# A token-MLP's first matmul split into eight and six column blocks instead of seven and seven

## The chip, the core and the metric

The kernel runs on one core of a Trainium2 chip. Time is the device time of one execution in microseconds (us), as the median of several runs; a profiled execution gives a trace of every instruction. Five engines matter here: TensorE (PE, with its weight loads shown as PEld) multiplies; VectorE (DVE) and ScalarE (ACT) do elementwise work and move results out of PSUM, the matmul's accumulators, which have eight banks; GpSimd (POOL) only builds constants; SyncE (SP) issues almost all DMA transfers, in order, from one queue.

## The reference

`x` is a [2048, 512] bf16 matrix. The result mixes a linear-attention block `a` and a token-mixing MLP `b` by a gate per row:

```python
g = _sigmoid((x * gate_w).sum(-1, keepdims=True))
# a: linear attention, 32 heads of 16
q, k, v = split(x @ wqkv)
phi = lambda t: jnp.where(t > 0, t + 1, jnp.exp(t)) + 1e-6
pq, pk = phi(q), phi(k)
kv = einsum("bhsd,bhse->bhde", pk, v);  z = einsum("bhsd->bhd", pk)
a = (pq @ kv / (pq . z + 1e-6)) @ wo
# b: layer norm, then an MLP along the 2048 rows
h = _layernorm(x)
u = gelu(einsum("bsd,sf->bdf", h, w1) + b1)     # w1: [2048, 1792]
y = einsum("bdf,fs->bds", u, w2) + b2           # w2: [1792, 2048]
b = y.transpose(0, 2, 1)
return g * a + (1 - g) * b
```

(`split` stands for the reference's reshape into q, k and v of 32 heads.) Note that the MLP mixes rows: its first matmul contracts over all 2048 rows of `h`, its second makes one output row out of 1792 hidden values.

## The kernel before

The 2048 rows are 16 row tiles of 128 (`NT`), the 512 features four blocks (`ND`), the 1792 hidden columns of w1 fourteen blocks of 128 (`NF`). Every large matmul is 128 x 128 weights against 512 columns and fills one PSUM bank. The code is written under a framework that keeps each engine's instructions in the order in which the program pins them, hands out PSUM banks from one pool of eight (`bank`, L70) and inserts the waits. So five orders are fixed by hand: TensorE's, VectorE's, ACT's, SP's queue and ACT's few DMAs.

TensorE's order is this.

- Warm-up matmuls (`warm_ps`) and a small one that turns the biases (`vps`, read by ACT at L229 and L230).
- **First MLP stage** (L266 to L277): while x and w1 stream in tile by tile, every row tile t is normalised (`ln_bn`, `ln_aggr`, `ln_apply` on VectorE, a square root on ACT) into `xh`, and TensorE adds its product with the first seven blocks of w1's columns to seven accumulators `accA`, all open at once. The last four row tiles (`TAIL`) are done accumulator by accumulator, so that each is finished and sent through gelu (L257, ACT) while the next one is being completed. Columns 0 to `FA` of w1 lie in `w1A`, the rest in `w1B`.
- **k stage** (L314 to L323): per row tile, four matmuls `kacc`, `phi` (an exp on ACT, two instructions on VectorE) into `pk`, and four tiles later four matmuls that add x^T pk to four accumulators `Gps`; VectorE adds up z. `Gps` goes to `G_sb` (L331). While the first MLP stage still runs, VectorE also does twelve of the sixteen dot products of the gate (`gate`, L252).
- **Second MLP stage** (L469): one block of w1's columns at a time (`mlp1_block`, 16 matmuls, accumulator `accB`), seven in all; behind the first four stand 3, 4, 4 and 5 tiles of q (`q_tile`, 4 matmuls and `phi` each), behind the first also the small kv matmuls, behind the second those of W2sb = kv wo. The accumulators of the first four blocks are kept until the q tiles are done, then gelu'd; ACT loads its gelu table once for this.
- **Last stage** (L540): for eight, four and three row tiles at a time the second matmul of the MLP (`y_mm`, 14 matmuls), then for each of those tiles the attention's part, 4 matmuls with weights from `pqT` (`a_mm`), and `finish` on ACT, and the store. The last row tile comes by itself in two parts.

Between q and the last stage lies a path without TensorE. `normalise(t)` (L388, four instructions on VectorE) divides phi(q) by its denominator and multiplies it by the gate's odds, then SP stores the tile to `q_dram`. After four tiles `turn(c)` (L408) reads it back as four DMA transposes into `pqT`. SP's queue from L500 on is, in order: the stores of tiles 0 to 3, the two loads of the second half of w2 (`load_w2(1, ...)`), turn(0), the stores of 4 to 7, turn(1), the stores of 8 to 11, turn(2), and then output stores mixed with the last four normalised tiles. `a_mm` of tiles 4c to 4c+3 needs turn(c).

w1A, w1B and the two halves of w2 share two slots of the pool `wstream`: the first half of w2 comes into the place of w1A, the second into that of w1B, when their last matmuls are done. `load_w2(0, ...)` stands in SP's queue behind the transposes of z (`z_out`, L361).

Of the kernel before, what the change touches and what calls it, by code (L numbers as in the profile page):

```python
# [11 lines left out]
BF16 = mybir.dt.bfloat16  # L12
# [4 lines left out]
def kernel(  # L17
# [14 lines left out]
    P = nc.NUM_PARTITIONS  # L32
# [7 lines left out]
    S, D = X.shape  # L40
    F = B_w1.shape[1]
    NT = S // P
    ND = D // P
    NF = F // P
    SC = 512
    NSC = S // SC
    assert S == 2048 and D == 512 and F == 1792
    NFA = NF // 2
    FA = NFA * P
    TAIL = 4  # L50

# [7 lines left out]
    gw_row_view = gate_w.rearrange("(o d) -> o d", o=1)  # L59

    persist = ctx.enter_context(tc.tile_pool(name="persist", bufs=1))
    wpool = ctx.enter_context(tc.tile_pool(name="wstream", bufs=2))
    work = ctx.enter_context(tc.tile_pool(name="work", bufs=3))
    dpool = ctx.enter_context(tc.tile_pool(name="dpool", bufs=1, space=bass.MemoryType.DRAM))
    psum = ctx.enter_context(tc.tile_pool(name="psum", bufs=8, space=bass.MemoryType.PSUM))
# [1 line left out]
    def ptile(shape, dt, name):  # L67
        return persist.tile(shape, dt, name=name, tag=name)

    def bank(name):  # L70
        return psum.tile([P, SC], FP32, name=name, tag="bank")
# [10 lines left out]
    wk_sb = ptile([P, ND, D], BF16, "wk_sb")  # L82
# [1 line left out]
    wo_sb = ptile([P, ND, D], BF16, "wo_sb")  # L84
    pqT = ptile([P, ND, S], BF16, "pqT")
    uT = ptile([P, NF, D], BF16, "uT")
    G_sb = ptile([P, ND, D], BF16, "G_sb")
    kvbdT = ptile([P, ND, P], BF16, "kvbdT")
    pq = ptile([P, NT, D], BF16, "pq")
    zb = ptile([P, D], FP32, "zb")  # L90
# [24 lines left out]
    nc.vector.memset(eps_t[:], EPS)  # L115


    w1A = wpool.tile([P, NT, FA], BF16, name="w1A", tag="w")
    w1B = wpool.tile([P, NT, FA], BF16, name="w1B", tag="w")

    pin = tc.keep_in_program_order

    def load(o, i, eng=None, **kw):
        pin((eng or nc.sync).dma_start(out=o, in_=i, **kw))
# [113 lines left out]
    def gate(t):  # L238
        junk = work.tile([P, D], BF16, name="junk", tag="junk", bufs=1)
        tc.keep_in_program_order(  # L240
            nc.vector.tensor_tensor_reduce(  # L241
                out=junk[:], in0=xr[:, t, :], in1=gw_b[:], scale=1.0, scalar=0.0,
                op0=ALU.mult, op1=ALU.add, accum_out=gpre[:, t : t + 1],
            )
        )


    def gate_odds(t0, t1):
        pin(nc.vector.tensor_scalar_min(out=gpre[:, t0:t1], in0=gpre[:, t0:t1], scalar1=60.0))
        pin(nc.scalar.activation(out=odds[:, t0:t1], in_=gpre[:, t0:t1], func=ACT.Exp))  # L250
# [6 lines left out]
    def gelu(acc, j):  # L257
        pin(
            nc.scalar.activation(
                out=uT[:, j, :], in_=acc[:], func=ACT.Gelu_apprx_tanh,  # L260
                bias=b1_sb[:, j : j + 1], scale=1.0,
            )
        )


    accA = [bank("accA") for _ in range(NFA)]  # L266

    def mlp1(acc, w, col, t, last):
        mm(acc[:], w[:, t, col : col + P], xh[:, t, :], t == 0, last)

    for t in range(NT - TAIL):
        for j in range(NFA):
            mlp1(accA[j], w1A, j * P, t, False)
    for j in range(NFA):
        for t in range(NT - TAIL, NT):
# [49 lines left out]
    def evict(o, acc, i):  # L325
        if i % 2 == 0:
            pin(nc.scalar.copy(out=o, in_=acc))
        else:
            pin(nc.vector.tensor_copy(out=o, in_=acc))

    for i in range(ND):  # L331
        evict(G_sb[:, i, :], Gps[i][:], i)
    pin(nc.vector.tensor_copy(out=z_parts[:, 0, :], in_=zacc[:]))
# [7 lines left out]
    def mlp1_block(j):  # L341
        acc = bank("accB")
        for t in range(NT):
            mlp1(acc, w1B, (j - NFA) * P, t, t == NT - 1)
        return acc

    def q_tile(t):
        qacc = bank("qacc")
        for k in range(ND):
            mm(qacc[:], xT[:, k, t * P : (t + 1) * P], wq_sb[:, k, :], k == 0, k == ND - 1)  # L350
        phi(pq[:, t, :], qacc)
# [14 lines left out]
    def z_row():  # L366
        pin(nc.vector.tensor_reduce(out=z_cols[:], in_=z_turned[:], op=ALU.add, axis=AX.X))
        load(zr_dram[:].rearrange("o (p j) -> p (o j)", p=P), z_cols[:])
        zm = persist.tile([P, D], FP32, name="z_mixed", tag="zacc")
        z_row_mixed.append(zm)  # L370
        load(zm[:], zr_dram[:].to_broadcast([P, D]))

    def z_order():
        pin(
            nc.scalar.copy(
                out=zb[:].rearrange("p (j c) -> p j c", j=ND),
                in_=z_row_mixed[0][:].rearrange("p (c j) -> p j c", j=ND),
            )
        )
# [36 lines left out]
    def kv_blocks():  # L416
        kvps = bank("kvps")
        for j in range(ND):
            for k in range(ND):
                for p in range(0, P, 64):  # L420
                    c = j * P + p
                    mm(kvps[p : p + 64, j * 64 : j * 64 + 64], wv_sb[:, k, c : c + 64],
                       G_sb[:, k, c : c + 64], k == 0, k == ND - 1, tile_position=(0, p))

        for j in range(ND):
            for p in range(0, P, 32):
                r = (p + 32 * j) % P
                pin(
                    nc.vector.tensor_tensor(
                        out=kvbdT[r : r + 32, j, p : p + 32],  # L430
                        in0=kvps[p : p + 32, j * 64 + p % 64 : j * 64 + p % 64 + 32],
                        in1=mask[p : p + 32, p : p + 32], op=ALU.mult,
                    )
                )

    def w2_blocks():
        w2ps = [bank("w2ps") for _ in range(ND)]
        for j in range(ND):
            for p in range(0, P, 32):
                r = (p + 32 * j) % P  # L440
                mm(w2ps[j][p : p + 32, :], kvbdT[r : r + 32, j, p : p + 32],
                   wo_sb[r : r + 32, j, :], True, True, tile_position=(r, p))
        for j in range(ND):
            evict(W2sb[:, j, :], w2ps[j][:], j)


    w2s = []

    def load_w2(h, f0):
        if f0 == 0:  # L450
            w2s.append(wpool.tile([P, NF, S // 2], BF16, name="w2h", tag="w"))
        load(
            w2s[h][:, f0 : f0 + 7, :],
            w2_view[:, f0 : f0 + 7, h * (S // 2) : (h + 1) * (S // 2)],
        )


    z_out()
    load_w2(0, 0)
    load_w2(0, 7)  # L460


# [3 lines left out]
    gates = [[], [12, 13], [14, 15], []]  # L466
    qi = 0
    waiting = []
    for b in range(NFA):  # L469
        acc = mlp1_block(NFA + b)  # L470
        waiting.append((acc, NFA + b))
        if b == 0:
            kv_blocks()
        if b == 1:
            w2_blocks()
        if b < QB:
            for _ in range(n_q[b]):
                q_tile(qi)
                qi += 1
            for t in gates[b]:  # L480
                gate(t)
            if b == 2:
                gate_odds(0, NT)
            if b == 1:
                z_row()
        if b == QB - 1:
            z_order()
        if b >= QB - 1:
            for a, j in waiting:
                gelu(a, j)  # L490
            waiting = []
# [8 lines left out]
    for t in range(12):  # L500
        normalise(t)
        if t == 3:
            load_w2(1, 0)
            load_w2(1, 7)
        if t % 4 == 3:
            turn(t // 4)
# [80 lines left out]
```

## Time and profile before

| what | value |
| --- | --- |
| median of 3 runs | 163.24 us (163.14 to 163.45) |
| profiled execution | 163.19 us, of it span 161.5 us from the first to the last instruction |
| granted TensorE clock | 1.000 |
| first matmul of accA to last store | 4.96 us to 161.5 us |
| first MLP stage (accA) | 4.96 to 29.3 us |
| k stage (kacc, Gps) | 29.3 to 57.0 us |
| second MLP stage and q | 57.0 to 96.2 us |
| last stage (yps) | 96.2 to 158.5 us |
| w1A: 15 loads of 224 KB, issue to landing | 4.2 us (median) |
| w2's halves: 4 loads of 1792 KB | 7.7 us (median) |
| pqT: 16 DMA transposes, issue to landing | 2.8 us (median) |

Stages are by the start of the first matmul of each. The trace models the end of a matmul: one is shown with some 379 ns although the next starts 216 ns after it, so starts are what to count. A timeline line gives start, length, engine, line of the code, operation, what it writes and reads, and how many instructions are merged in it; a "q" behind an engine's name means its queue (waits and DMA issues). Helpers record all matmuls at L75 and all DMA issues at L124, so tiles' names tell them apart.

### The profile page before, as it was taken

What the parts mean: (1) busy time and instruction counts of PE and PEld (TensorE: products, weight loads), DVE (VectorE), ACT (ScalarE), POOL (GpSimd) and SP (SyncE); (2) the same over time, 40 slices, a digit from 0 to 9 for tenths busy, and PEclk for the clock granted to TensorE, in tenths of its full rate; (3) what the DMA queues carried; (4) which work ended last, traced back from release to release, by engine and by line L of the source; (5) the groups of instructions that cost most, each with busy time, mean ns of one, the idle gap of its engine ahead of it and who ended that gap; (6) DMA issues with size and microseconds to landing.
All of it is one profiled execution on the core that took longest, in us unless ns stands there. A gap on an engine that the chain in (4) does not pass through costs nothing.

```text
span 161.5 us, 2192 instructions
## 1 busy us (share of the span) xinstructions
PE 156.9 (97%) x775; PEld 73.0 (45%) x789; DVE 117.6 (73%) x272; ACT 53.1 (33%) x91; POOL 1.5 (1%) x10
## 2 busy tenths in 40 slices
PE   7999999999999999999999999999999999999992
PEld 5444444444444445444444444444444444444452
DVE  2999989999999997998959999999999900000002
ACT  3222258962332124261348730000008330150140
POOL 3000000000000000000000000000000000000000
PEclk9999999999999999999999999999999999999999
DMA  4999996445699942169930103999445367360021
GB/s 139 279 351 341 335 186 139 108 105 102 165 394 380 265 136 81 37 211 381 334 67 0 39 32 80 345 392 296 153 69 162 91 196 233 71 189 4 0 97 33
DMA packets 36806, 28.33 MB, mean 175 GB/s; under 512 B 20412, under 2 KB 33084, under 8 KB 36796
## 3 DMA queue, kind: packets, MB, share of 16 engines
q1 hardware_dynamic: 36320, 27.90, 58.7%
q10 hardware_dynamic: 476, 0.30, 0.6%
q8 instruction: 6, 0.10, 0.3%
q14 instruction: 4, 0.03, 0.1%
HBM read 19.28 MB, written 4.46 MB: 147 GB/s over the span
## 4 chain that ended last, share of the span: by engine, by line
PE 97%; issue 1%; DVE 0%; DVEq 0%
PE yps L75 38%; PE accA L75 15%; PE accB L75 15%; PE qacc L75 9%; PE kacc L75 9%; PE Gps L75 8%; PE warm_ps L75 2%; PE kvps L75 0%; DVE ot L531 0%; PE w2ps L75 0%; PE vps L75 0%; DVEq L531 0%
## 5 line engine op out<-in xcount | busy, mean ns | idle before, releaser
L75 PE MATMUL yps<-uT,w2h 128*128 128x512 bf16 (+2 forms) x234 | 49.0, 366 | 0.2
L75 PEld LDWEIGHTS <-w2h 128*128 128x128 bf16 x238 | 22.8, 98 | 25.9
L524 ACT ACTIVATE ot<-yps,c,c 128x512 bf16<-128x512 f32 x15 | 11.5, 777 | 46.9 <-DVE pq L400 24.4
L75 PE MATMUL accB<-xh,w1B 128*128 128x512 bf16 x110 | 24.9, 379 | 0.1
L75 PE MATMUL accA<-xh,w1A 128*128 128x512 bf16 x110 | 24.4, 381 | 0.1
L531 DVE TENSOR_SCALAR ot<-yps,c,c 128x384 bf16<-128x384 f32 (+1 forms) x2 | 1.1, 544 | 29.0 <-PE yps L75 29.0
L75 PEld LDWEIGHTS <-xT 128*128 128x128 bf16 x128 | 12.4, 98 | 14.9 <-issue 0.2
L75 PEld LDWEIGHTS <-w1B 128*128 128x128 bf16 x112 | 10.9, 98 | 13.2
L75 PEld LDWEIGHTS <-w1A 128*128 128x128 bf16 x112 | 10.9, 98 | 13.2 <-issue 0.4
L75 PE MATMUL kacc<-wk_sb,xT 128*128 128x512 bf16 x63 | 15.7, 379 | 0.1
L75 PE MATMUL Gps<-pk,xr 128*128 128x512 bf16 x62 | 15.5, 379 | 0.1
L75 PE MATMUL yps<-W2sb,pqT 128*128 128x512 bf16 (+2 forms) x67 | 14.6, 366 | 0.1
L75 PE MATMUL qacc<-wq_sb,xT 128*128 128x512 bf16 x62 | 14.4, 379 | 0.1
L282 ACT ACTIVATE e<-qacc 128x512 bf16<-128x512 f32 x16 | 9.6, 597 | 12.2 <-PE qacc L75 8.0
L282 ACT ACTIVATE e<-kacc 128x512 bf16<-128x512 f32 x16 | 9.2, 598 | 12.7 <-PE kacc L75 7.0
L196 DVE BATCH_NORM_STATS2 stats<-xr 128x6 f32<-128x512 bf16 (+1 forms) x19 | 11.1, 582 | 2.1 <-DMA xr<-in_A_x_dram 2.1
L400 DVE SCALAR_TENSOR_TENSOR pq<-pq,odds,rd 128x512 bf16<-128x512 bf16 x16 | 12.0, 752 | 0.6
L396 DVE TENSOR_REDUCE den<-prod 128x32 f32<-128x544 f32 x16 | 11.5, 720 | 0.6
L289 DVE SCALAR_TENSOR_TENSOR pk<-kacc,e 128x512 bf16<-128x512 f32 x16 | 11.1, 692 | 1.0
L289 DVE SCALAR_TENSOR_TENSOR pq<-qacc,e 128x512 bf16<-128x512 f32 x16 | 11.1, 692 | 0.6
L241 DVE CUSTOM_DVE_ANT_0 junk<-xr,gw_b 128x512 bf16<-128x512 bf16 x16 | 11.0, 690 | 0.5
L284 DVE TENSOR_SCALAR e<-e 128x512 bf16<-128x512 bf16 x32 | 9.2, 288 | 2.8 <-ACT e L282 2.4
(54 smaller groups left out, 95.3 us busy)
## 6 DMA issues: line engine op xcount, KB each, us to landing
w2h<-in_B_w_dram SPq DMA_DIRECT2D x4, 1792.0 KB, 7.7
w1B<-in_B_w_dram SPq DMA_DIRECT2D x4, 896.0 KB, 8.3
w1A<-in_B_w_dram SPq DMA_DIRECT2D x15, 224.0 KB, 4.2
xr<-in_A_x_dram SPq DMA_DIRECT2D x16, 128.0 KB, 3.9
q_dram<-pq SPq DMA_DIRECT2D x16, 128.0 KB, 1.8
out_dram<-ot SPq DMA_DIRECT2D x15, 128.0 KB, 1.8
wk_sb<-in_A_wqkv_dram SPq DMA_DIRECT2D x1, 512.0 KB, 7.0
wv_sb<-in_A_wqkv_dram SPq DMA_DIRECT2D x1, 512.0 KB, 13.5
```

The lines of the kernel that those rows point to most:

```text
L75: nc.tensor.matmul(o, lhsT=lhsT, rhs=rhs, start=start, stop=stop, **kw)
L196: pin(nc.vector.bn_stats(out=stats[t][:, h, :], in_=xr[:, t, d0:d1]))
L241: nc.vector.tensor_tensor_reduce(out=junk[:], in0=xr[:, t, :], in1=gw_b[:], scale=1.0, scalar=0.0, op0=ALU.mult, op1=ALU.add, accum_out=gp ...
L282: pin(nc.scalar.activation(out=e[:], in_=acc[:], func=ACT.Exp))
L284: nc.vector.tensor_scalar(out=e[:], in0=e[:], scalar1=1.0, scalar2=PHI_EPS, op0=ALU.min, op1=ALU.add)
L289: nc.vector.scalar_tensor_tensor(out=o, in0=acc[:], scalar=0.0, in1=e[:], op0=ALU.max, op1=ALU.add)
L396: pin(nc.vector.tensor_reduce(out=den[:], in_=prod[:], op=ALU.add, axis=AX.X))
L400: nc.vector.scalar_tensor_tensor(out=heads, in0=heads, scalar=odds[:, t : t + 1], in1=rd[:].unsqueeze(2).to_broadcast([P, NH, HEAD]), op0= ...
L524: nc.scalar.activation(out=ot[:, d0:d1], in_=yps[:, d0:d1], func=ACT.Identity, scale=c1[:, t : t + 1], bias=c2[:, t : t + 1],)
L531: nc.vector.tensor_scalar(out=ot[:, d0:d1], in0=yps[:, d0:d1], scalar1=c1[:, t : t + 1], scalar2=c2[:, t : t + 1], op0=ALU.mult, op1=ALU.add,)
```

## The change

The first MLP stage works on eight blocks of w1's columns with eight open accumulators, the second on the remaining six. `w1A` grows to 1024 columns (256 KB per row tile instead of 224) and `w1B` shrinks to 768. The two slots of `wstream` become two tags with a slot each: `w1st` for w1A and then w2's first half (32 KB per partition instead of 28), `w2nd` for w1B and then w2's second half (28 KB, as before). The 4 KB come from `G_sb`, which no longer has a place of its own but is made, where it is first written, in the place of `wk_sb`, the weights of the k stage. The loop of the second stage runs over six blocks; which q tiles, gates and other parts stand behind block b is as it was, so two blocks instead of three come after the last q tile.

```diff
-    NFA = NF // 2
+    NFA = 8
     FA = NFA * P
...
-    wpool = ctx.enter_context(tc.tile_pool(name="wstream", bufs=2))
+    wpool = ctx.enter_context(tc.tile_pool(name="wstream", bufs=1))
...
-    G_sb = ptile([P, ND, D], BF16, "G_sb")
...
-    w1A = wpool.tile([P, NT, FA], BF16, name="w1A", tag="w")
-    w1B = wpool.tile([P, NT, FA], BF16, name="w1B", tag="w")
+    w1A = wpool.tile([P, NT, FA], BF16, name="w1A", tag="w1st")
+    w1B = wpool.tile([P, NT, F - FA], BF16, name="w1B", tag="w2nd")
...
+    G_sb = persist.tile([P, ND, D], BF16, name="G_sb", tag="wk_sb")
     for i in range(ND):
         evict(G_sb[:, i, :], Gps[i][:], i)
...
-            w2s.append(wpool.tile([P, NF, S // 2], BF16, name="w2h", tag="w"))
+            w2s.append(wpool.tile([P, NF, S // 2], BF16, name="w2h", tag=("w1st", "w2nd")[h]))
...
-    for b in range(NFA):
+    for b in range(NF - NFA):
         acc = mlp1_block(NFA + b)
```

## The prediction, made before the change was run

> **What bounds the kernel now.** I read the page first (busy shares, the chain of waits), then the timeline of SP's queue, then TensorE's own timeline stage by stage.
>
> ```profile
> span 161.5 us, 2192 instructions
> PE 156.9 (97%) x775; PEld 73.0 (45%) x789; DVE 117.6 (73%) x272; ACT 53.1 (33%) x91; POOL 1.5 (1%) x10
> ...
> PE 97%; issue 1%; DVE 0%; DVEq 0%
> ```
>
> The chain that ends last is TensorE from 0.83 us to 158.5 us, with no other engine in it until the last store. A busy TensorE could still hide pauses, so I took starts, not durations: the 48 matmuls of the last three blocks of the second stage start from 85.79 to 96.15, which is 10.36/48 = 0.2158 us each, and the same spacing holds in every other stage. From 5.13 to 157.4 us TensorE never really waits. The change leaves the number of matmuls as it is (14 blocks of 16 either way), so it can win only what the head loses: the first matmul of accA waits for the first normalised tile (4.96 until the second starts at 5.35 instead of 5.18, 0.17 us), and the 29th starts 0.253 after its predecessor, 0.04 us late. Nothing else is to be had. The question is what the reordering makes late.
>
> The one place where data arrive just in time is the read of pqT in the last stage:
>
> ```profile
> 96.09 2.87 SPq L124 DMA_DIRECT2D q_dram<-pq  x2
> 99.05 1.07 SPq L124 DMA_DIRECT2D w2h<-in_B_w_dram  x2
> 100.48 10.98 SPq L124 DMA_TRANSPOSE pqT<-q_dram  x4
> 111.50 2.06 SPq L124 DMA_DIRECT2D q_dram<-pq  x4
> 114.96 6.29 SPq L124 DMA_TRANSPOSE pqT<-q_dram  x4
> 121.30 2.05 SPq L124 DMA_DIRECT2D q_dram<-pq  x4
> 124.75 5.03 SPq L124 DMA_TRANSPOSE pqT<-q_dram  x4
> ```
>
> This is SP's queue in order of time (start, length, what, how many). A line of four transposes is one turn(c). Turn(1), issued from 114.96, feeds tiles 4 to 7. Its four landings are at 117.56, 120.61, 121.10 and 122.78 (issue plus its own time to landing). Against it stands the timeline of TensorE's weight loads:
>
> ```profile
> 120.11 6.79 PEld L75 LDWEIGHTS <-pqT 128*128 128x128 bf16 x32
> ```
>
> Its 32 loads are 0.2159 apart ((6.79 - 0.10)/31), so tile 4 (loads 17 to 20) wants its four pieces at 123.57, 123.78, 124.00 and 124.21. The tightest margin is 1.43 us, at tile 4's fourth piece; every other one of this stage is 2.9 us or more.
>
> **The change, part by part.** *Eight blocks first.* 16 matmuls (block 8) move from the second stage to the first: 16 x 0.2158 = 3.45 us. Everything from the first kacc to the last qacc starts 3.45 us later. From y_mm on TensorE is where it was, since b = 6 of the second loop is gone: after the last qacc stand two blocks (6.91 us) instead of three (10.36).
>
> *The head.* Per row tile w1A has 256 KB instead of 224, so up to w1A of tile 1 64 KB more go ahead. At the 300 GB/s of 5.5 to 6.5 us that is 0.21 us: it landed at 6.54 and lands at 6.75. Its load is wanted at about 6.80 (5.35 + 7 x 0.216, less the 0.06 of a load ahead of its matmul), a wait of -0.05 to 0.15 us; I take 0.0. Later tiles have slack: 384 KB per tile at 345 GB/s are 1.11 us against 8 x 0.2158 = 1.73 us of TensorE, and a tile's layer norm on VectorE repeats every 1.18 us. The 0.04 us pause of the 29th matmul goes. Head: between -0.04 and +0.15, taken as 0.
>
> *Banks.* warm_ps, vps and seven accA are nine tiles for eight banks now; with ten, one accA must take over vps's bank, free once ACT's two copies of L229 and L230 are done at 5.93; its first matmul is due no earlier than 6.43. kacc then starts on the bank of accA[0], whose gelu (24.46 now, 2.6 later then) ends some 5 us before. The later rows: gelu of block 7 from 32.99, the table load 1.28, exp 0.60, then VectorE's 0.29 and 0.69 put pk(0) at 36.6; Gps wants it at 33.65 + 3.45 = 37.1. VectorE's gates, which end at 32.3 now, are off that path. Cost 0; if the 0.5 us of cover went, each 0.1 over it would be 0.1 on the end.
>
> *G in wk's place.* It waits for the last reader of wk_sb. The kacc matmuls end 4.3 us ahead of the last Gps (52.81 against 57.13 in the chain), and G is evicted only after Gps. Cost 0; the waits on ACT's and VectorE's queues behind it are the same ones as now.
>
> *w1B and the w2 halves.* w1B is 3.1 MB instead of 3.7 MB, starts some 1.5 us later (0.5 MB more ahead of it at 345 GB/s), ends where it did, and is wanted 3.45 us later. w2's first half is released by SP's transposes of z behind the Gps stage: 3.45 us later, in by about 85 (81.7 now, when the small transfer behind it had landed), wanted at 96.15. The row of z (z_mixed in at 85.02, wanted by ACT's copy at 86.49) moves as a whole. The second half goes where w1B was, free at 96.15 as now.
>
> *Gelus ahead of y_mm.* zb, the table load and the gelus of blocks 8 to 12 (88.91 to 91.91 now) move to 92.4 to 95.4; TensorE wants the first at 97.88. The gelu of the last block is at 96.36 either way. Cost 0, with 2.5 us of cover.
>
> *The normalise chain.* This is the part that is not covered. VectorE starts normalise(0) at 88.39, after the phi of the last qacc, which TensorE's qacc sets; so it starts at 91.84. A tile takes 2.53 us and VectorE has no pause until 128.9, so every q_dram is 3.45 us later. On SP stands behind the store of tile 3 (98.63, waiting for VectorE) first the load of w2's second half, then turn(0), the stores of 4 to 7, turn(1). That whole row moves by 3.45 us. Turn(0) then lands at 117.1, wanted at 120.11: covered. Turn(1) is issued from 118.41.
>
> How long does turn(1) take? Now 6.29 us to issue; turn(2), the same bytes, took 5.03, and the views of the tile pqT over these two stretches give
>
> ```profile
> DMA to landing us min/median/max: 2.6/3.2/4.5
> ...
> DMA to landing us min/median/max: 2.5/2.7/2.7
> ```
>
> (the first line is turn(1), the second turn(2)).
> The packet records say why: at 118.16 one 16 KB packet of the instruction queue occupies one DMA engine for 1.37 us, in the middle of turn(1). The queue's last two packets are 27.65 us apart, the time in which TensorE starts 256 instructions (128 pairs of 0.2158), so it follows TensorE's count and stays at 118.16. The last packet of the stores before turn(1) is at 114.59, hence at 118.04 then: the fetch falls between the stores and the transposes (first data at 116.20 + 3.45 = 119.65, the fetch over at 119.53). So turn(1) then has turn(2)'s rhythm: landings 2.54, 3.83, 5.21 and 6.51 after the first issue, at 120.95, 122.24, 123.62 and 124.92. The fourth is wanted at 124.21; with 0.04 from landing to load (the w1A wait at 6.58) TensorE stops for 0.75 us.
>
> [...]
>
> The bounds for this stall: 0 if SP's row gains 0.75 us, 2.06 if turn(1) keeps its present rhythm (122.78 + 3.45 + 0.04 - 124.21). I take 0.75, since the position of the fetch follows from rows. What is later is covered: turn(2) landed at 131.26 and is wanted at 139.11, turn(3) at 143.92 against 151.63, w2's second half was in by 112.1 (turn(0), behind it in the queue, had landed) and is wanted at 128.53; each moves by 3.45 at most.
>
> **Sum.** Profiled execution 163.19 us (span 161.5 and 1.7 around it), head 0, stall +0.75: 163.94. The median is 163.24, 0.05 above the profiled run: 164.0 us.
>
> **Rivals.** *Turn(1) is still hit by the fetch.* The gap between 118.04 and 118.16 is 0.12 us; a DMA row 0.15 later or a fetch 0.15 earlier puts a store behind the 1.37 us packet, SP waits for that store, and the transposes start up to 1.4 later. For it: the small gap, and ten tiles in eight banks may shift TensorE's count by a wait or two. Against: both times follow TensorE. Stall 2.06: 165.3 us.
>
> *No stall: w2's load makes it up.* This one ends on the other side.
>
> ```profile
> 100.00:104.00 4.00, 3.95 (x19) 1.84 (x19) 3.86 (x7) 0.00 (x0) 0.00 (x0) 1.00 0.83 266
> 104.00:108.00 4.00, 4.00 (x20) 1.79 (x19) 3.79 (x8) 0.00 (x0) 0.00 (x0) 1.00 1.05 395
> ```
>
> The last two columns are the share of the DMA engines and GB/s. Were the first of these stretches as fast as the second, the load would save (395 - 266) x 4 / 395 = 1.3 us; from 0.75 us on nothing waits, and the time is 163.2. Against it: the load has the engines to itself both now and after, so I see no reason for another pace.
>
> *pk(0) is late.* If ACT loads a second table behind the last gelu (1.28 us, 0.8 over the cover of 0.5), Gps waits 0.8 us on top: 164.8. Against it, one load stands there now, and the functions are the same. *Faster:* only the head's 0.04 to 0.2 us without a stall, 163.0 to 163.2; to pass 0.2% it would need more than the head holds.
>
> **Chances.** Forecast 0.55, fetch hits 0.27, no stall 0.10, late pk(0) 0.04, faster 0.04. A measurement of this kernel tells 0.2% (0.33 us) from no change. Slower: the forecast, the fetch and pk(0), 0.86; within 0.2%: 0.11, the no-stall case and a little of the faster one; faster 0.03. The range goes from a stall of 0.3 (163.5) to the fetch case with 0.2 for the head (165.5).
>
> **What would show it.** Right: the only new wait of TensorE on a DMA is a weight load of pqT near 124.2, 0.75 us long, at tile 4's last piece; normalise starts near 91.8; kacc starts near 32.8. A wait of 2 us there with a late store speaks for the fetch. Wrong: no pause of pqT, or TensorE waiting anywhere before 96 us.

## The result and the profile after

The changed kernel takes 164.21 us (median of 8 runs, 163.9 to 165.01) against 163.34 us for the kernel before (8 runs, 163.13 to 163.88): a ratio of 1.0057, 95% interval 1.0039 to 1.0075, or 0.93 us slower (0.64 to 1.23; the medians lie 0.87 apart). The profiled execution took 164.22 us, its span is 162.5 us instead of 161.5. The granted clock is 0.998 against 1.000.

From the page of the changed kernel, the span, the busy shares and the shares of the chain that ends last:

```profile
span 162.5 us, 2208 instructions
PE 157.6 (97%) x789; PEld 73.0 (45%) x789; DVE 117.8 (72%) x272; ACT 53.2 (33%) x91; POOL 1.5 (1%) x10
...
PE 71%; DVE 18%; DMA 5%; SPq 2%; issue 1%; ACTq 1%; ACT 0%; DVEq 0%
```

The busy shares are as good as unchanged and show nothing. The chain does: it was TensorE for 97%, now a quarter of it is put down to VectorE, SP's queue and DMAs. Where it comes back to TensorE is in the pieces of the chain in order of time (start, length, what):

```profile
101.40 0.75 DVE pq L401
...
111.51 0.75 DVE pq L401
...
116.19 0.36 DVE rd L399
...
116.66 1.78 DMA q_dram<-pq
...
118.46 1.35 SPq L123
...
119.86 1.25 SPq L123
...
121.16 1.26 SPq L123
...
122.47 2.92 DMA pqT<-q_dram
...
125.43 34.12 PE yps L75 x175
```

Read from below: TensorE's last 34 us hang on the fourth transpose of pqT, that one on SP's issue of the three before it (1.25 to 1.35 us each), these on the store of tile 7, which went out at 116.66 as the last of the four stores. Above the store the chain misleads, because it infers who released whom: the `rd` at 116.19 belongs to tile 9, while normalise(7) had ended with the `pq` at 111.51 (0.75 long). The four stores waited for SP's own row. Normalise(3) ended with the `pq` at 101.40, SP issued that tile's store at 102.18, then the load of w2 and turn(0) up to 114.96, then the four stores. So VectorE's late start reaches turn(1) through tile 3 and what stands behind it on SP, and VectorE's 18% is too much.

SP's queue, then TensorE's matmuls before and after, from the timelines:

```profile
102.18 0.33 SPq L123 DMA_DIRECT2D q_dram<-pq  x1
102.60 1.07 SPq L123 DMA_DIRECT2D w2h<-in_B_w_dram  x2
104.03 10.93 SPq L123 DMA_TRANSPOSE pqT<-q_dram  x4
115.00 2.06 SPq L123 DMA_DIRECT2D q_dram<-pq  x4
118.46 5.26 SPq L123 DMA_TRANSPOSE pqT<-q_dram  x4
```

```profile
120.33 7.07 PE L75 MATMUL yps<-W2sb,pqT 128*128 128x512 bf16 x31
```

```profile
120.43 4.26 PE L75 MATMUL yps<-W2sb,pqT 128*128 128x512 bf16 x19
125.43 2.98 PE L75 MATMUL yps<-W2sb,pqT 128*128 128x512 bf16 x13 [0.74 <-DMA pqT<-q_dram]
```

(One of the 32 matmuls has no record in the profile before.) From the load on, each line of SP's row is 3.50 to 3.55 us later than it was (99.05, 100.48, 111.50, 114.96), only turn(1) is quicker to issue, 5.26 us instead of 6.29. In the changed kernel TensorE stops before its 20th matmul with pqT, the fourth of tile 4. The figure in brackets, 0.74, is short of the truth, because a matmul is shown with 379 ns of which the next one overlaps all but 216. By starts, the 19th is at 124.315 and the 20th at 125.431: 1.116 - 0.216 = 0.90 us. From the first matmul of the last stage to the last of the kernel TensorE takes 62.149 us in the profile before and 63.059 now, 0.91 more. So the stall is the whole of the last stage's loss; the rest of the span's 1.0 us is 0.10 that stood on the clock already when the last stage began (96.257 instead of 96.154), and that comes from the head.

### The profile page after: what moved, and what is told of

Read it like the earlier page. It is cut to its first block, busy times and chain, and to the rows that moved or that the text cites. A ratio compares the mean times of both kernels' runs of the same rounds, so it can differ in the third digit from the quotient of the medians.

```text
span 162.5 us, 2208 instructions
## 1 busy us (share of the span) xinstructions
PE 157.6 (97%) x789; PEld 73.0 (45%) x789; DVE 117.8 (72%) x272; ACT 53.2 (33%) x91; POOL 1.5 (1%) x10
## 4 chain that ended last, share of the span: by engine, by line
PE 71%; DVE 18%; DMA 5%; SPq 2%; issue 1%; ACTq 1%; ACT 0%; DVEq 0%
PE yps L75 21%; PE accA L75 17%; PE kacc L75 9%; PE accB L75 9%; PE Gps L75 9%; PE qacc L75 7%; DVE den L397 4%; DVE pq L401 4%; DVE prod L392 4%; SPq L123 2%; DVE rd L399 2%; DVE pq L288 2%; DMA b_rows<-in_B_b_dram 2%; DMA pqT<-q_dram 2%; DMA q_dram<-pq 1%
## 5 line engine op out<-in xcount | busy, mean ns | idle before, releaser
L75 PE MATMUL accA<-xh,w1A 128*128 128x512 bf16 x128 | 27.8, 379 | 0.0
L75 PE MATMUL accB<-xh,w1B 128*128 128x512 bf16 x96 | 21.5, 379 | 0.0
L75 PEld LDWEIGHTS <-w1A 128*128 128x128 bf16 x128 | 12.4, 98 | 14.9
L75 PEld LDWEIGHTS <-w1B 128*128 128x128 bf16 x96 | 9.4, 98 | 11.3
```

The source lines that it names most:

```text
L75: nc.tensor.matmul(o, lhsT=lhsT, rhs=rhs, start=start, stop=stop, **kw)
```

## The experiments

One figure serves for all of them: the time from the first matmul of `yps` to the kernel's last matmul, by the traces' starts. Where nothing stalls it is 62.149 or 62.150 us, whatever happened before.

**The chain alone.** The kernel before, with VectorE held up ahead of normalise(0):

```diff
     pin(nc.vector.tensor_tensor(out=c2[:], in0=c1[:], in1=b2_sb[:], op=ALU.mult))
+    for t in range(5):
+        gate(t)
```

> The kernel before, split 7 + 7, in which VectorE repeats five of the gate's dot products (5 x 0.73 = 3.67 us, no effect on the result) just ahead of normalise(0); nothing else differs. Theory (the loss of the change is turn(1) coming 3.45 us later than tile 4 of the last stage allows): normalise starts near 92.1 us, turn(1) is issued near 118.6 and its last piece lands near 125.4, wanted at 124.2; TensorE waits 1.1 to 1.4 us for pqT there and nowhere else, time 164.4 to 164.8, ratio 1.007 to 1.009. Rival (the loss comes from eight open accumulators, the larger pieces of w1A and the moved tiles): none of these is in this kernel, so no wait on pqT, 163.3, ratio 1.000.

164.86 us against 163.35, ratio 1.0071 (1.0049 to 1.0094), a little over the expected time. TensorE's timeline in it:

```profile
120.91 4.39 PE L75 MATMUL yps<-W2sb,pqT 128*128 128x512 bf16 x19
126.13 2.98 PE L75 MATMUL yps<-W2sb,pqT 128*128 128x512 bf16 x13 [0.83 <-DMA pqT<-q_dram]
```

The same stop at the same matmul, in a kernel with seven open accumulators and every tile in its old place. Normalise began at 92.52, turn(1) was issued from 119.39, its last piece landed at 126.09; the last stage took 63.281 us, 1.13 more than without a stall (0.11 of it before the 19th matmul, for the third piece). The rest by which this profile is longer is its head: the last stage began at 96.74 instead of 96.15. A late normalise chain is enough to make the loss.

**The tiles alone.** The changed kernel with the split put back; G in wk's place and the two separate slots stay.

```diff
-    NFA = 8
+    NFA = NF // 2
```

> The changed kernel with the split put back to 7 + 7: what is left of the change is G in wk's place and a slot each for the two column ranges. Theory (the split alone moves the normalise chain): no wait on pqT, 163.3, ratio 1.000 within 0.002. Rival (the moved tiles carry part of the cost, through a wait for wk's last reader or another place in SBUF): above 163.6.

163.46 us against 163.31, ratio 1.0004 (0.999 to 1.0017), the last stage 62.149 us, no wait for pqT. The moved tiles cost nothing that can be measured.

**The load out of turn(1)'s way.** The changed kernel with one of the two big loads further up in SP's queue:

```diff
-        if t == 3:
+        if t == 0:
             load_w2(1, 0)
+        if t == 3:
             load_w2(1, 7)
```

> The changed kernel with SP's queue reordered: the first of the two loads of w2's second half goes ahead of the store of tile 1, free to start when w1B is released at 96.3 us, the second stays ahead of turn(0). Theory (turn(1) is late because the whole 3.5 MB load stands in its row behind normalise(3)): the load no longer ends last, turn(1) waits only for normalise(7) near 112.1 and is issued near 114 instead of 118.5, last piece by 121 to 122, wanted at 124.3; no wait on pqT, time 163.3 to 163.5, ratio 1.000 to 1.001 (0.1 us of the head stays). Rival (normalise itself is too late, or the last stage is short of something else): the wait for pqT stays at about 1.1 us, 164.2, ratio 1.006.

163.27 us against 163.35, ratio 0.999 (0.9978 to 1.0002). SP's queue and TensorE's matmuls:

```profile
96.19 0.39 SPq L123 DMA_DIRECT2D w2h<-in_B_w_dram  x1
96.86 5.39 SPq L123 DMA_DIRECT2D q_dram<-pq  x3
102.31 0.43 SPq L123 DMA_DIRECT2D w2h<-in_B_w_dram  x1
105.04 5.33 SPq L123 DMA_TRANSPOSE pqT<-q_dram  x4
110.41 2.05 SPq L123 DMA_DIRECT2D q_dram<-pq  x4
113.86 5.04 SPq L123 DMA_TRANSPOSE pqT<-q_dram  x4
```

```profile
120.17 7.07 PE L75 MATMUL yps<-W2sb,pqT 128*128 128x512 bf16 x32
```

Normalise is as late as in the changed kernel (91.69), but the first load uses the time from 96.19 on in which the DMA engines had been nearly idle (busy share 0.12 from 96.2 to 102.6 in the changed kernel); turn(1) goes out 4.6 us earlier, and all 32 matmuls run in one piece. So normalise being 3.45 us later is not what stopped TensorE by itself: it was late together with 3.5 MB that stood in the same queue behind it.

**The same edit before the change.** The edit just shown, on the kernel before.

> The kernel before, split 7 + 7, with the first load of w2's second half ahead of the store of tile 1. Theory (with cover enough behind the second stage the split itself is worth nothing, TensorE being full either way): no wait on pqT before or after, 163.2 to 163.4, ratio 1.000, the same as the split 8 + 6 with this edit. Rival (the split 8 + 6 gains a few tenths at the head, where eight matmuls a tile ease the layer norm): this kernel is slower by 0.2 us or more than the split 8 + 6 with the same edit.

163.40 us against 163.31, ratio 1.0007 (0.9995 to 1.002), the last stage 62.149 us. With this edit the split 8 + 6 (0.999) and the split 7 + 7 (1.0007) lie 0.0017 apart, some 0.28 us, and their intervals overlap only just. The rival's 0.2 us for 8 + 6 is thus neither shown nor excluded: the two were measured against different runs of the kernel before, and by the profiles their last stages are equal while their heads, which vary with the execution (last section), differ by 0.25 us. What can be said is that neither differs from the kernel before by more than the measurement tells.

**The cover given back.** The changed kernel with q in three blocks, so that three MLP blocks again follow the last q tile:

```diff
-    QB = 4
-    n_q = [3, 4, 4, 5]
-    gates = [[], [12, 13], [14, 15], []]
+    QB = 3
+    n_q = [5, 5, 6]
+    gates = [[], [12, 13], [14, 15]]
```

> The changed kernel with the sixteen q tiles behind the first three blocks of the second stage (5, 5 and 6) instead of the first four (3, 4, 4 and 5): again three blocks stand between the last q tile and the last stage, as in the kernel before. Theory (the cover that the change took from the normalise chain is what is missing): the last q tile ends near 86 us again, normalise starts between 88.5 and 89.5 (z's row, in at 88.1, may hold it for 1 us), turn(1)'s last piece lands 2.5 to 3.5 us before it did, no wait on pqT, time 163.3 to 163.5, ratio 1.000 to 1.001. Rival (the denser q tiles overload VectorE or the banks): TensorE waits in the second stage instead, by 0.5 us or more, 163.9 or above.

163.70 us against 163.35, ratio 1.0026 (1.0007 to 1.0046): better than the change, yet the expected start of normalise was missed. VectorE's timeline shows why:

```profile
87.70 0.69 DVE L288 SCALAR_TENSOR_TENSOR pq<-qacc,e 128x512 bf16<-128x512 f32 x1
88.31 0.68 DVE L240 CUSTOM_DVE_ANT_0 junk<-xr,gw_b 128x512 bf16<-128x512 bf16 x1
...
89.04 0.69 DVE L240 CUSTOM_DVE_ANT_0 junk<-xr,gw_b 128x512 bf16<-128x512 bf16 x1
...
91.23 0.69 DVE L392 TENSOR_TENSOR prod<-pq,zb 128x512 f32<-128x512 bf16 x1 [0.33 <-ACT zb L376]
```

Two gate products now stood between the last phi and normalise, and ACT, in its order, made the odds from them (89.98) before it copied z (90.10). Normalise began only 0.7 us earlier than in the changed kernel, and the stall shrank to 62.442 - 62.149 = 0.29 us. I had counted the q tiles and forgotten what is queued behind them.

With the gates one block earlier as well:

```diff
+    gates = [[12, 13], [14, 15], []]
...
-            if b == 2:
+            if b == 1:
                 gate_odds(0, NT)
```

> The changed kernel with the q tiles behind three blocks (5, 5, 6), and now also the last four gate products and the odds one block earlier, so that no VectorE work stands between the last q tile and normalise(0); in the run before this one, where they stood there, normalise started at 91.2 and the wait on pqT was 0.5 us. Theory (what counts is when normalise starts): it starts near 90.0, held by ACT's copy of z whose row is in at 88.8; turn(1)'s last piece lands near 123.5 to 124.0, wanted at 124.2 to 124.4; a wait of 0.1 us or none, 163.3 to 163.5, ratio 1.000 to 1.001. Rival (the wait is set by something else, such as the load of w2): it stays at 0.5 us or more.

163.57 us against 163.31, ratio 1.0009 (0.9997 to 1.002). Now only the copy of z holds it:

```profile
90.42 0.69 DVE L392 TENSOR_TENSOR prod<-pq,zb 128x512 f32<-128x512 bf16 x1 [1.12 <-ACT zb L376]
```

Turn(1) was issued from 117.16, its last piece landed at 124.50 and was wanted at 124.69; the last stage took 62.150 us. Counted back from the first matmul of the last stage, normalise begins 4.2, 4.3, 5.4 and 6.2 us ahead of it in the chain-alone kernel, the changed one and these two; the stall falls with it (1.13, 0.91, 0.29, 0).

**The fetch.** The changed kernel with 18 TensorE instructions fewer ahead, so that the fetch which came at 118.33 us comes later:

```diff
-    one = nc.const_aps.tensor(1.0, [P, 256], BF16)
-    for _ in range(18):
-        mm(warm_ps[:, :256], one[:, 0:P], one, True, True)
+    one = nc.const_aps.tensor(1.0, [P, 512], BF16)
+    for _ in range(9):
+        mm(warm_ps[:, :512], one[:, 0:P], one, True, True)
```

> The changed kernel with 9 warm-up matmuls of 512 columns in place of 18 of 256: the same columns, 18 instructions fewer on TensorE, so each block of its instructions is fetched 18 x 0.108 = 1.9 us later, the fetch at 118.3 us then at about 120.3. Theory (the fetch's packet holds up the transposes it meets; in the changed kernel it falls just ahead of turn(1)'s data): it now falls among turn(1)'s packets, turn(1) takes some 6.3 us to issue instead of 5.26, its last piece lands near 126.4, TensorE waits about 2.1 us for pqT instead of 1.1, time 165.0 to 165.4, ratio 1.010 to 1.013. Rival (the fetch does not matter for the transposes, their pace is given by something else): the wait stays at 1.1 us, 164.2, ratio 1.006.

164.39 us against 163.35, ratio 1.0066 (1.0045 to 1.0088); the last stage 63.143 us, a stall of 0.99 instead of 0.91. The expected 1 us more did not come; the stall and the time are as the rival had them. The view of the tile pqT over turn(1) in this kernel, ahead of it the same view of the changed kernel:

```profile
DMA to landing us min/median/max: 2.5/2.8/2.9
```

```profile
DMA to landing us min/median/max: 2.7/3.5/4.4
```

The fetch (from 120.78, reckoned for about 120.3) did meet the transposes: the first piece landed 4.4 us after its issue instead of 2.5. But the later pieces made up most of it, and only the last one counts: turn(1) took 7.14 us instead of 6.92. Over all profiles, from the packet records and the landings:

| kernel | turn(1) issued from | fetch from, length | first issue to last landing |
| --- | --- | --- | --- |
| before | 114.96 | 118.16, 1.37 | 7.82 |
| changed | 118.46 | 118.33, 1.07 | 6.92 |
| chain alone (7 + 7, late normalise) | 119.39 | 119.01, 1.29 | 6.70 |
| tiles alone (7 + 7) | 115.16 | 118.89, 1.49 | 8.09 |
| load early (8 + 6) | 113.86 | 118.58, 0.88 | 7.15 |
| load early (7 + 7) | 113.95 | 118.70, 0.92 | 7.17 |
| q in three | 117.68 | 118.62, 1.30 | 7.43 |
| q in three, gates earlier | 117.16 | 118.88, 1.05 | 7.34 |
| fetch later | 118.41 | 120.78, 0.92 | 7.14 |
| load early, bias row early | 114.47 | 118.94, 1.14 | 7.16 |
| load early, 20 warm-ups | 114.86 | 119.37, 0.92 | 7.43 |
| turn(2), before and changed | 124.75, 127.21 | none | 6.51, 6.52 |

(The last two kernels are described below. Turn(2), which meets no fetch, takes 6.50 to 6.69 us over all eleven profiles.)

In the two profiles in which the fetch begins before turn(1), turn(1) takes 6.7 and 6.9 us; in the nine in which it falls inside, 7.1 to 8.1, that is 0.5 to 1.5 more than turn(2). The two longest packets (1.37 and 1.49) stand beside the two longest turns (7.82 and 8.09). Below that the packet's length does not decide: 0.92 stands beside 7.14, 7.17 and 7.43. So the fetch goes with a cost for the transposes, mostly of half to nine tenths of a microsecond; the 1.3 us of the profile before was near the upper end. Only the kernel with the later fetch moves it on purpose; the other rows are found, not set.

**Two tries to beat both.** The early load together with the second bias row ahead of w1A's first piece on ACT's queue, since the matmul on the biases waited 0.3 us for that row in the profile of the changed kernel:

```diff
-    load(w1A[:, 0, 0:P], w1_view[:, 0, 0:P], nc.scalar)
     load(b_rows[NF : NF + NT, :], b2_view, nc.scalar)
+    load(w1A[:, 0, 0:P], w1_view[:, 0, 0:P], nc.scalar)
```

> The changed kernel with two edits: the first load of w2's second half ahead of the store of tile 1, which removed the wait on pqT, and the second bias row ahead of the first piece of w1A on ACT's queue, since the matmul on the biases waited for it by 0.3 us in the profile of the changed kernel. Theory (the late bias row delays the first matmul of accA): it starts at 4.95 or earlier and the time is 163.1 to 163.3, ratio 0.998 to 0.999. Rival (the first matmul waits for the normalised tile and for the clock, not for the row): no difference from the kernel with the first edit alone, ratio 0.999 to 1.000.

163.54 us against 163.31, ratio 1.0009 (0.9996 to 1.0021): no gain. `accA` began at 4.95, as the theory had it, but then waited 0.47 us for w1A of tile 1, which landed at 7.10. And the early load with two more warm-up matmuls:

```diff
-    for _ in range(18):
+    for _ in range(20):
```

> The changed kernel with the first load of w2's second half ahead of the store of tile 1 (no wait on pqT) and 20 warm-up matmuls instead of 18, a try for a version that beats both kernels. In five of the profiles the first one to four matmuls of accA start 0.39 to 0.43 us apart, twice the 0.216 of all others, after a pause of 0.3 to 0.7 us behind the warm-up. Theory (the pause lets TensorE fall to half rate): two more warm-up matmuls leave a pause under 0.3 us, all of accA's matmuls start 0.216 apart, and the time is 163.0 to 163.2, ratio 0.997 to 0.999. Rival (the half rate comes and goes with the execution, whatever stands ahead, and the head also waits for w1A of tile 1): ratio 0.999 to 1.001, no gain over 18.

163.42 us against 163.44, ratio 0.9991 (0.9979 to 1.0003): again no gain, and the half rate was still there, as the rival had it: the pause ahead of accA was under 0.3 us, yet its first five matmuls start 0.30 to 0.43 us apart. Nothing run here beats the kernel before by more than the measurement can tell.

## Why the prediction was right, and where it was off

Forecast: 164.0 us, one stall of 0.75 us at the fourth piece of tile 4. Measured: 164.21 us, one stall of 0.90 us at that piece.

- *The shift.* Forecast 3.45 us for all from kacc to the last q. Normalise began at 91.94 (forecast 91.84), turn(1) at 118.46 (118.41). Right; this execution's head was 0.10 us later, of which turn(1) kept 0.05.
- *The cause of the stall.* The kernel before with nothing but a late normalise shows it; the changed kernel with the load moved, or with normalise early enough (90.4), does not. Shown from both sides.
- *The size of the stall.* Two terms were wrong and in part cancelled. Turn(1) was to take 6.51 us from first issue to last landing, like turn(2); it took 6.92 and was issued 0.05 later, so the last piece came at 125.38 and not at 124.92: 0.46 more. Of this, 0.23 is the first transpose's issue (1.35 us instead of 1.12). The forecast compared the fetch with the transposes' data alone, and there it was right: the fetch was over at 119.40, the first data moved after 119.6. But the issue began inside the fetch, by the forecast's own times too (118.41, the fetch until 119.53), and that was put at nothing. The chain-alone kernel, the other one whose issue began inside the fetch, has 1.32; that the fetch is the reason is likely, not shown. The last 0.18 is the fourth piece, which landed 2.92 us after its issue instead of 2.74; why is open. Against that, I counted the stall from when the weight load was due. In the trace a load starts one matmul ahead of its own (the first for pqT at 120.11 us, its matmul at 120.33, in the profile before), so TensorE stops only 0.22 us later: 0.22 less. The late head moved the due times by another 0.10. 0.75 + 0.46 - 0.22 - 0.10 = 0.89.
- *The fetch as a rival.* Priced at 2.06 us of stall on the ground that turn(1) would keep its rhythm of 7.82. With the fetch put into turn(1) on purpose the stall was 0.99. The price was one execution's; the table has 7.14 to 8.09. And the choice between the two cases was closer than the forecast argued: in the nine profiles of kernels with the same count of TensorE instructions the fetch begins 22.0 to 22.6 us after the last stage does, a spread of 0.6 us, where the forecast relied on a gap of 0.12. That it fell clear of the data here (22.07) was in part luck.
- *No stall.* The load was not quicker (103.05 to the last landings of turn(0) at 117.12 against 99.50 to 113.63: 14.07 and 14.13 us from the second load's issue). This rival fell as argued.
- *Banks, G, gelus, z's row, turn(2), turn(3).* No wait of TensorE on any of them; the only new ones are for pqT and 0.3 us for the bias row. Right.
- *The head.* Forecast 0; in this execution 0.10, but not for the reason weighed: w1A of tile 1 landed at 6.65 and was not waited for, the bias row at 5.02 was (4.72 before). `accA` began 0.29 us later for it and got 0.19 back, having no matmul at half rate. And the reading of the 0.17 us before accA's second matmul as a wait for the normalised tile was wrong: the last section says what it is.

## What to carry to other kernels

An engine that is full can still lose when work is moved ahead on it (here 0.93 us, with TensorE busy for 97% of the span): every chain that starts where the moved work used to end starts later, while its reader stays. Look for the reader with the smallest margin behind a queue that is served in order, and count everything that stands in that queue between the late item and the reader; moving one load out of that row can be worth more than the time that the chain is late (here 4.6 us against 3.45). Measure a stall of TensorE by starts of matmuls (here 0.90 us), not by its idle time (0.74) and not by the due time of a weight load.

## What the runs showed of the hardware

**The first matmuls run at half rate, for a time that changes with the execution.** The 18 warm-up matmuls of 256 columns start 0.213 us apart, which is the spacing of 512 columns at full rate (0.216). In the profile before, one matmul of accA still takes 0.38 us; in the changed kernel none; in the chain-alone kernel four start 0.40 to 0.43 us apart. TensorE's instructions in the same stretch of the head, in the chain-alone kernel and in the changed one (columns: stretch, its length, TensorE busy and number, clock, DMA share, GB/s):

```profile
4.90:7.00 2.10, 2.10 (x7) 1.00 0.88 289
```

```profile
4.90:7.00 2.10, 1.85 (x10) 1.00 0.83 264
```

Seven instructions against ten, and the clock column says 1.00 in both. Taken over all profiles, the change to full rate comes between 3.6 us (the last warm-up matmuls of the tiles-alone kernel start 0.14 and then 0.11 apart) and some 6.8 us (the kernel with 20 warm-ups), that is 2.8 to 6.0 us after the first matmul (at 0.84), and each late matmul costs 0.2 us. The traces' own clock records, of which the column gives a mean, begin with full speed at 4.04 us in the early-load kernel, 4.81 in the changed one, 6.63 in the chain-alone one and 6.75 with 20 warm-ups, in agreement with the spacing. Together with w1A of tile 1, which in the tiles-alone kernel landed 0.65 us too late, this moved the start of the last stage between 96.00 and 96.74 us among the ten profiles whose TensorE has the same work up to there (97.01 with the two warm-ups more). It is nearly as large as the effect under study, and may be why single runs of one kernel lie 0.7 us apart or more; the runs without a profile cannot show it.

**A fetch of TensorE's instructions can take a DMA engine for 0.88 to 1.49 us** (the fifth of the six 16 KB packets of the instruction queue, in the table above), and four DMA transposes into which it falls took 0.5 to 1.5 us longer than four that met none. It moves with TensorE's count of instructions: with 18 instructions fewer the fifth fetch came at 120.78 instead of 118.33, 2.45 us later, where 1.9 were reckoned; the difference is within the 0.6 us by which its place varies between executions.
